# Turned key sums on column tiles in their own PSUM bank, one copy for both output banks, and input loads that begin one step earlier

## Chip, cores and metric

The kernel runs on one core of one Trainium2 chip. The metric is the device time of one execution in microseconds (us); lower is better. Three runs of the kernel before gave 825.5, 828.97 and 832.24 us, median 828.97.

## What is computed

Linear attention over 8 sequences, 8 heads, 576 tokens and 64 channels, followed by a layer that sends each token to one of 8 experts. The attention part, which is the part the change touches:

```
def phi(x):
    proj = einsum('bhsd,df->bhsf', x, w_phi)              # 64 -> 128 features
    proj = proj - max(abs(proj), axis=-1)
    return concat([exp(proj), exp(-proj)], axis=-1)       # 256 features
q_p, k_p = phi(q), phi(k)
kv  = einsum('bhsf,bhsd->bhfd', k_p, v)
z   = sum(k_p, axis=2)
out = einsum('bhsf,bhfd->bhsd', q_p, kv) / (einsum('bhsf,bhf->bhs', q_p, z)[..., None] + 1e-6)
```

Then x is the output with the heads side by side (512 channels). The logits of a token are x @ w_gate (8 experts) and its local gate is x @ w_local (1 column). The expert e is the argmax of the logits, or the expert of the token before where the local gate is 0.5 or more; the output row is p[e] * (relu(x @ w1[e]) @ w2[e]).

## The kernel before

**Tiling.** The work of the attention is cut into 16 units (a pair of sequences and a pair of heads), each of 9 chunks of 128 tokens, 144 chunks in all; two chunks make a pair, 72 pairs. Chunk 4 of a unit holds the end of one sequence and the start of the next, so a unit has two sums of keys and values (`kvp`), one for each sequence: 32 sums.

**Rounds.** After a short head (pairs 0 to 2) and one step for pair 3 alone (`step`), `round` (lines 676 to 718) runs 34 times on two pairs, a and b (`cur`), while it finishes the two pairs of the round before (`prev`). TensorE's order is the order in which this function is written. In one round TensorE does:

1. `qtr` of prev's first pair: turns its projected queries into `tq`; `products` of pair a into `pj` (line 423); `qtr` of prev's second pair.
2. The turns: for each sum that was finished since the last round, four transposes (`halves`, line 448) of its 128 value columns `kvs[:, sg, MID]` into columns 256 to 383 of the `pj` tile that pair b will be written to (`fb`), and VectorE copies them out as `ks` (line 527).
3. `products` of pair b into that tile.
4. `sums` of prev's first pair (lines 479, 493) into `kvp`.
5. `num` (line 568) twice: the output of two finished pairs, one after the other, into the two banks of one tile `nm` of two banks. After each, ScalarE copies its bank to `nx` (line 573), VectorE makes the reciprocals `rc` (lines 575, 576), GpSimd multiplies into `xo` (line 578) and adds the gate columns to `lg` (lines 587 to 590), and SyncE writes `xo` to the tensor `xs` in HBM (line 593).
6. The gates of the sums turned in step 2: `ks` times `wgi` (line 535) into columns 256 to 291 of pair a's `pj` tile (`fa`), copied by ScalarE into nine columns at each end of `kvs` (line 537). Only after this is a sum ready for `num`.
7. `sums` of prev's second pair. When a sum has its fifth part, `kv_end` has ScalarE copy it from `kvp` to `kvs` (lines 514, 515).

Between these stand `chores`: steps of the routing (`gate`), of a table, and of the first experts' weights, whose halves ScalarE casts (line 644) and GpSimd subtracts (line 646) in the last ten rounds or so.

**The other engines in a round.** VectorE: for each of a and b a maximum (line 430) and a subtraction (line 432), about 1.2 us each. ScalarE: four exponentials of `tq` (`qexp`, line 462), then four of the keys (line 440), two for the pair b of the round before and two for pair a. ScalarE's place for the copies at high priority is chosen by the scheduler.

**PSUM.** `pj` has two tiles (`psf`), `kvp` two (`pskv`), and `tq` and `nm` share one tile of two banks (`psb`, one buffer): `qtr` of the next round waits until `nm` has been copied out, and `num` until `qexp` has read `tq`.

**Loads.** Keys and queries come in `kq` (four buffers) and values in `v` (five), three chunks to a load. Groups 0 to 3 are asked for at the start, the rest is a list `loads` in the order keys, queries, values. `paced_load` issues one of them per chunk, four per round, each held on SyncE's queue until a given matmul is done:

```
if self.loads and NBP * NHP * NC - 12 - len(self.loads) < at - 4:
    self.hold(self.loads.pop(0)(), behind)
```

The first is popped in the first round (at = 8), so load number k (from 0) goes out at chunk k + 8 and belongs to group 4 + k // 3, whose first chunk is 12 + 3 (k // 3): keys go out four chunks ahead of the products that read them, queries three.

**After the rounds.** `last_turns` and `last_sums` (lines 720 to 757) finish the last two pairs and the outputs that are left; then the expert part runs, about 430 us of it, in which TensorE is busy nearly all the time.

Of the kernel before, what the change touches and what calls it, by code (L numbers as in the profile page):

```python
# [21 lines left out]
TB = 2 * S  # L22
# [44 lines left out]
class Kernel:  # L67
# [9 lines left out]
    def run(self):  # L77
        nc, tc, A = self.nc, self.tc, self.A
        act, dve = self.act, self.dve
        with ExitStack() as root:  # L80
# [49 lines left out]
            with tc.manual_schedule(engines={mybir.EngineType.PE}):  # L130
                self.head()
                self.step(HEAD)
                pairs = ExitStack()
                self.psb = self.mkpool(pairs, "psb", 1, "left", PSUM)
                prev = (HEAD,)
                for p in range(HEAD + 1, n // 2, 2):
                    if p == FILL + 4:
                        self.background.append(self.table())
                    self.round((p, p + 1), prev)
                    prev = p, p + 1  # L140
                turn = self.last_turns(prev)
            pairs.close()
            self.psb = self.mkpool(back, "psb", 2, "left", PSUM)
            self.tail = True
            with tc.manual_schedule(engines={mybir.EngineType.PE}):
                self.last_sums(prev, turn)
            for x in self.background:
                for _ in x:
                    pass
# [35 lines left out]
    def fill(self, k):  # L185

        a, b = 17 * k // 4, 17 * (k + 1) // 4
        if k == 0:
            self.empty = self.back2.tile([128, 17, PLACE], F32, name="empty", tag="xo", bufs=4)
# [318 lines left out]
    def kv_end(self, u, b, t):  # L508


        hp = u % NHP
        kvs = self.back2.tile([128, 2, 2 * (KV + D + 1)], F32, name="kvs", bufs=4)
        with self.tc.high_priority():
            self.act.copy(kvs[:, :, MID].rearrange("p s (h d) -> p s h d", h=2), t[:, :, :, 0:D])
            self.act.copy(kvs[:, :, DEN], t[:, :, :, D])
        e = {}
# [12 lines left out]

        def gate(t):  # L530

            g = t[:, 0, 256:292].rearrange("p (s h e) -> p s h e", s=2, h=2)
            for sg in (0, 1):
                for r in (slice(0, 64), slice(64, 128)):
                    self.pe.matmul(g[r, sg], e["ks"][:, sg, r], self.wgi[:, hp], start=True, stop=True)
            with self.tc.high_priority():
                self.act.copy(kvs.rearrange("p s (h x) -> p s h x", h=2)[:, :, :, 0:9], g)
            self.kvb[u, b] = kvs
            self.gated.add((u, b))
            while self.pair < NBP * NHP * NC // 2 and self.batches(2 * self.pair) | self.batches(2 * self.pair + 1) <= self.gated:  # L540
                self.ready.append(self.pair)
                self.pair += 1
        self.turns.append(turn)
# [3 lines left out]
        u, c = divmod(i, NC)  # L547
        return {(u, int(c > 4)), (u, int(c > 3))}

    def num(self, t):  # L550

        if not self.ready:
            return
        dve, pool = self.dve, self.pool
        j = self.ready.pop(0)
        t = t[:, 0:4 * KV].rearrange("p (c k) -> p c k", c=2)
        spans = []
        for z in (0, 1):
            u, c = divmod(2 * j + z, NC)
            qp = self.ch.pop(2 * j + z)["qp"]  # L560
            spans.append((u, c, slice(z, z + 1)))
# [8 lines left out]
        if spans[0][0] == spans[1][0]:  # L570
            spans = [(u, spans[0][1], slice(0, 2))]
        nx = self.back2.tile([128, 2, 2 * KV], F32, name="nx", bufs=2)
        self.act.copy(nx, t)  # L573
        rc = self.back2.tile([128, 2, 2], F32, name="rc", bufs=3)
        dve.tensor_scalar_add(rc, nx[:, :, DEN], 1e-6)
        dve.reciprocal(rc, rc)
        xo = self.back2.tile([128, 2, 2 * KV], F32, name="xo", bufs=4)
        pool.tensor_mul(xo.rearrange("p c (h k) -> p c h k", h=2), nx.rearrange("p c (h k) -> p c h k", h=2),  # L578
                        rc.unsqueeze(3).broadcast_to([128, 2, 2, KV]))
        for u, c, z in spans:  # L580
            bp, hp = divmod(u, NHP)
            n = z.stop - z.start
            if hp == 0 and c == 0:
                self.lg[bp] = self.back2.tile([128, NC, 9], F32, name="lg")
            lg, ga, gb = self.lg[bp][:, c:c + n], xo[:, z, 0:9], xo[:, z, 2 * KV - 9:2 * KV]
# [5 lines left out]
            r0 = bp * TB + c * 128  # L591
            dst = self.xs[r0:r0 + n * 128, hp * 128:hp * 128 + 128].rearrange("(c p) d -> p c d", p=128)
            self.sp.dma_start(dst, xo[:, z, MID])
            if c + n == NC and hp == NHP - 1:
                self.ends(bp)

# [53 lines left out]

    def sums(self, p):

        for i in sorted((2 * p, 2 * p + 1), key=lambda i: i % NC != 4):
            if i % NC == 4:
                self.kv4(i)
            else:
                self.kv(i)

    def step(self, p):

        exps = self.proj(p)
        exps()
        pj = self.ch[2 * p - 2]["pj"]
        self.qtr(p - 1, pj)
        self.qexp(p - 1, pj)
        self.sums(p - 1)
        self.exps = lambda: None

    def ask(self):

        if self.asked:
            self.asked()
            self.hold(self.marks[self.sp], self.last_num)
            self.asked = None

    def round(self, cur, prev):

# [7 lines left out]
        fa, fb = [x.rearrange("p h c j f -> p h (c j f)") for x in (ta, tb)]  # L685
# [29 lines left out]
        if prev[1:]:  # L715
            self.sums(prev[1])
        self.paced_load(2 * b + 1, self.last_sum)
        self.ask()

    def last_turns(self, prev):  # L720

        t = self.psb.tile([128, 2, 512], F32, name="tq", tag="nm")
        for k, p in enumerate(prev):
            self.qtr(p, t, 256 * k)
        pj = self.psf.tile([128, 2, 512], F32, name="pj")
        turns, self.turns = self.turns, []
        for x in [x(pj) for x in turns]:
            x(pj)
# [4 lines left out]
        self.sums(prev[0])  # L733
        return pj

    def spread(self, n):
        for _ in range(n):
            self.num(self.psb.tile([128, 512], F32, name="nm"))

    def last_sums(self, prev, pj):  # L740

        self.spread(1)
        gates, self.gates = self.gates, []
        for x in gates:
            x(pj)
        self.chores()
        self.sums(prev[1])
        self.spread(2)
        t = self.psf.tile([128, 2, 512], F32, name="pj")
        turns, self.turns = self.turns, []  # L750
        for x in [x(t) for x in turns]:
            x(t)
        self.spread(max(len(self.ready) - 1, 0))
        gates, self.gates = self.gates, []
        for x in gates:
            x(t)
        self.spread(len(self.ready))

    def chores(self):
# [1007 lines left out]
```

## Time and profile before

| | |
|---|---|
| median of 3 runs | 828.97 us (825.5 to 832.24) |
| the profiled execution | 830.83 us |
| its span in the profile | 829.1 us, so 1.73 us lie around the span |
| TensorE busy | 735.1 us, 89% of the span |
| VectorE, ScalarE, GpSimd busy | 477.0, 364.5, 286.0 us |
| the 34 rounds | from 15.9 to 384.6 us |
| the expert part | from 399.5 us to the end |

A busy share is a mean over stages with different limits; the rounds and the expert part have to be read apart. In the timeline a row merges neighbouring instructions of one kind: start, length in us, engine, line, operation, output and inputs, count, and in brackets the idle time before and what ended it. PEld is TensorE loading its stationary operand, which overlaps its matmuls.

### The profile page before, as it was taken

The page shows a single profiled execution, that of the slowest core. Times are in us where ns is not written, and L with a number is a line of the kernel's source. Part 1 is how long each engine was busy: PE and PEld are TensorE (multiplying, and loading weights), DVE is VectorE, ACT ScalarE, POOL GpSimd, SP SyncE. Part 2 cuts the span into 40 slices and gives each one's busy share as a digit, 9 for nine tenths or more (in the row PEclk, how much of TensorE's full clock was granted, in tenths as well). Part 3 has the DMA queues.
Part 4 walks back from the last instruction along what each step waited for, and adds up shares of the span by engine and source line. Part 5 has one row for each costly group of instructions (what it writes and reads, how often), then busy time and mean ns, then how long its engine had stood idle before and what let it go on. Part 6 is the DMA issues. An engine that isn't in the chain of part 4 may idle for free. (4 is left out here: it accounts for less than half of the span.)

```text
span 829.1 us, 22143 instructions
## 1 busy us (share of the span) xinstructions
PE 735.1 (89%) x9193; PEld 641.0 (77%) x9193; DVE 477.0 (58%) x862; ACT 364.5 (44%) x736; POOL 286.0 (34%) x448
## 2 busy tenths in 40 slices
PE   8678778778777777768999999999999999999997
PEld 7567777777677676668889888957897889788895
DVE  6454655764566655775675547265557556563520
ACT  5444554564455565456243533163333424342420
POOL 1202221244312464656774515240415142432011
PEclk9888999999899898999999999999999999999999
DMA  4633333343333454554343859986477558665630
GB/s 139 205 82 88 112 104 103 105 124 87 99 104 105 113 158 135 168 159 137 80 156 110 300 137 327 339 311 194 147 194 238 126 196 203 193 165 153 190 128 36
DMA packets 101143, 129.53 MB, mean 156 GB/s; under 512 B 41938, under 2 KB 80274, under 8 KB 100990
## 3 DMA queue, kind: packets, MB, share of 16 engines
q1 hardware_dynamic: 92560, 105.10, 43.5%
q0 software_dynamic: 8032, 22.78, 8.1%
q8 instruction: 73, 1.20, 0.6%
q14 instruction: 30, 0.25, 0.1%
q10 hardware_dynamic: 448, 0.20, 0.1%
HBM read 98.12 MB, written 21.80 MB: 145 GB/s over the span
## 5 line engine op out<-in xcount | busy, mean ns | idle before, releaser
L423 PE MATMUL pj<-first,kq 64*128 64x128 f32 x1120 | 94.5, 304 | 59.5 <-DVE ks L527 39.2
L430 DVE TENSOR_REDUCE m<-pj 128x8 f32<-128x1024 f32 x70 | 85.7, 1224 | 83.1 <-PE pj L423 82.2
L423 PEld LDWEIGHTS pj<-first,kq 64*128 64x128 f32 x1120 | 76.7, 201 | 69.2 <-DVE ks L527 43.3
L1458 PE MATMUL l<-xhi,whi 128*128 128x352 f32 (+5 forms) x352 | 124.1, 353 | 0.2 <-DVE hl L1505 0.2
L1460 PE MATMUL l<-xhi,wlo 128*128 128x352 f32 (+5 forms) x352 | 123.6, 351 | 0.0
L1459 PE MATMUL l<-xlo,whi 128*128 128x352 f32 (+5 forms) x352 | 123.4, 351 | 0.0
L1504 ACT ACTIVATE hh<-l 128x384 fp32r<-128x384 f32 (+4 forms) x88 | 45.0, 511 | 166.3 <-PE l L1460 166.1
L1282 DVE TENSOR_TENSOR wlo<-wraw,whi 128x1024 fp32r<-128x1024 f32 x80 | 99.9, 1265 | 29.0 <-ACT whi L1279 28.9
L568 PE MATMUL nm<-kvs,qp 128*64 128x74 f32 x2304 | 93.9, 238 | 21.7 <-ACT nx L573 20.4
L1458 PE MATMUL l<-whi,hh 128*128 128x512 f32 (+1 forms) x288 | 112.7, 391 | 0.0
L1459 PE MATMUL l<-wlo,hh 128*128 128x512 f32 (+1 forms) x288 | 112.3, 390 | 0.0
L1460 PE MATMUL l<-whi,hl 128*128 128x512 f32 (+1 forms) x288 | 112.2, 390 | 0.0
L1505 DVE SCALAR_TENSOR_TENSOR hl<-l,hh 128x384 fp32r<-128x384 f32 (+4 forms) x88 | 51.1, 580 | 102.8 <-ACT hh L1504 102.8
L568 PEld LDWEIGHTS nm<-kvs,qp 128*64 128x64 f32 x2304 | 85.4, 145 | 27.5 <-ACT nx L573 25.3
L578 POOL TENSOR_TENSOR xo<-nx,rc 128x296 f32<-128x296 f32 x72 | 49.0, 681 | 149.5 <-ACT nx L573 75.2
L462 ACT ACTIVATE qp<-tq 128x512 f32<-128x512 f32 x138 | 71.3, 602 | 65.3 <-PE tq L448 65.2
L1279 ACT CAST whi<-wraw 128x1024 fp32r<-128x1024 f32 x80 | 81.7, 1045 | 20.3 <-PE l L1460 12.8
L432 DVE TENSOR_TENSOR sb<-pj,m 128x1024 f32<-128x1024 f32 x70 | 85.5, 1221 | 3.7
L479 PE MATMUL kvp<-v,kp 128*64 128x65 f32 x2048 | 86.4, 243 | 0.0
L479 PEld LDWEIGHTS kvp<-v,kp 128*64 128x64 f32 x2048 | 76.3, 155 | 6.1 <-issue 2.2
L440 ACT ACTIVATE kp<-sb 128x512 f32<-128x512 f32 x140 | 78.2, 649 | 2.8 <-DVE sb L432 2.7
L1574 POOL DMA_INDIRECT out<-y,p_tokm x32 | 39.8, 1243 | 108.5 <-DVE y L1570 97.7
(273 smaller groups left out, 1065.1 us busy)
## 6 DMA issues: line engine op xcount, KB each, us to landing
wraw<-in_w1h SPq DMA_DIRECT2D x40, 512.0 KB, 4.9
wraw<-in_w2h SPq DMA_DIRECT2D x40, 512.0 KB, 4.5
kq<-in_kqT SPq DMA_DIRECT2D x88, 192.0 KB, 2.7
v<-in_va SPq DMA_DIRECT2D x48, 195.0 KB, 2.8
xs<-xo SPq DMA_DIRECT2D x64, 128.0 KB, 2.2
whi<-in_w2h SPq DMA_DIRECT2D x8, 512.0 KB, 5.5
wlo<-in_w2h SPq DMA_DIRECT2D x8, 512.0 KB, 6.2
wraw<-in_w1h SPq DMA_DIRECT2D x8, 256.0 KB, 2.8
```

The lines of the kernel that those rows point to most:

```text
L423: self.last_pe = self.pe.matmul(t[:, h, i % 2, j, :], kq[r, j, s], self.w2[r], start=True, stop=True)
L430: dve.tensor_reduce(m, f, AX.X, ALU.max, apply_absolute_value=True)
L432: self.last_dve = dve.tensor_sub(sb.rearrange("p h c j f -> p (h c j) f"), f, m.unsqueeze(2).broadcast_to([128, 8, 128]))
L440: self.last_act = act.activation(kp[:, :, :, sg, :].rearrange("p c h f -> p h c f"), sb[:, :, :, 0], AF.Exp, scale=1.0 - 2 * sg)
L462: self.last_act = self.act.activation(qp[:, sg].rearrange("p h (c r k) -> p (h c) r k", c=2, r=2), src, AF.Exp, scale=1.0 - 2 * sg)
L479: self.last_sum = self.pe.matmul(t[r, sg, h], kp[:, h, sg, r], v[:, h], start=first and sg + h == 0, stop=last and sg + h == 2)
L568: self.last_num = self.pe.matmul(t[r, z, k], qp[:, sg, h, q], self.kvb[u, int(c > 4 - x)][:, sg, k], start=sg == 0, stop=sg == 1)
L1279: self.act.copy(hi, raw)
L1282: (low or self.dve).tensor_sub(lo[:, c], raw[:, c], hi.bitcast(F32)[:, c])
L1458: mm(o, ah, bh, start=first, stop=False)
L1459: mm(o, ah, bl, start=False, stop=False)
L1460: self.last_pe = mm(o, al, bh, start=False, stop=last)
```

## The change

- `turn` writes the turned sum into the sum's own `kvp` bank, columns 0 to 255 (line 524 of the new kernel): four matmuls of `kvs` against the identity, each with all 128 partitions in and 64 out, in place of four transposes into pair b's `pj` tile. ScalarE, not VectorE, copies it to `ks` (line 526).
- `gate` writes into the same bank (line 534), and ScalarE copies from there (line 536).
- In a round, `turn` and `gating` now stand at two places each: turns behind `products` of b, with their gates behind the sums of prev's first pair; and turns behind the first `num`, with their gates behind the second.
- `num` only does the matmuls. A new `numbers` empties both banks of `nm` with one ScalarE copy straight into `xo` (592 elements, line 574), makes the reciprocals of both pairs at once, multiplies in place on GpSimd, and issues the write to `xs` ahead of the additions to `lg`. `nx` is gone; `xo` has three buffers of four chunks in place of four of two.
- The two chunks of prev's second pair are summed with the chores between them.
- `step` issues three loads, held behind its products; the pacing rule is as it was, so each later load goes out three chunks earlier (load k at chunk k + 5).
- `last_turns` and `last_sums` follow the same order.

```diff
-        def turn(t):
+        def turn():
+            ks = e["ks"] = self.back2.tile([128, 2, 128], F32, name="ks")
             for sg in (0, 1):
-                self.halves(t, 256 + sg * 64, kvs[:, sg, MID])
+                for x in (0, 1):
+                    r = slice(64 * x, 64 * x + 64)
+                    self.pe.matmul(o[r, sg * 128:sg * 128 + 128], kvs[:, sg, MID][:, r], self.ident, start=True, stop=True)
+            with self.tc.high_priority():
+                self.act.copy(ks.rearrange("p s k -> p (s k)"), o[:, 0:256])
             self.gates.append(gate)
-            return copy
-
-        def copy(t):
-            e["ks"] = self.back2.tile([128, 2, 128], F32, name="ks")
-            with self.tc.high_priority():
-                self.dve.tensor_copy(e["ks"].rearrange("p s (r k) -> p s r k", r=2),
-                                     t[:, :, 256:384].rearrange("p r (s k) -> p s r k", s=2))
-
-        def gate(t):
-
-            g = t[:, 0, 256:292].rearrange("p (s h e) -> p s h e", s=2, h=2)
+
+        def gate():
+
+            g = o[:, 0:36].rearrange("p (s h e) -> p s h e", s=2, h=2)
...
-        nx = self.back2.tile([128, 2, 2 * KV], F32, name="nx", bufs=2)
-        self.act.copy(nx, t)
...
+    def numbers(self, t, js):
...
+        xo = self.back2.tile([128, 4, 2 * KV], F32, name="xo", bufs=3)[:, 0:2 * w]
+        self.act.copy(xo.rearrange("p (n c) k -> p n (c k)", n=w), t[:, 0:w, 0:4 * KV])
+        rc = self.back2.tile([128, 4, 2], F32, name="rc", bufs=3)[:, 0:2 * w]
...
+        pool.tensor_mul(x, x, rc.unsqueeze(3).broadcast_to([128, 2 * w, 2, KV]))
...
     def step(self, p):
 
         exps = self.proj(p)
         exps()
+        for _ in range(3):
+            self.hold(self.loads.pop(0)(), self.last_pe)
...
         self.paced_load(2 * a, self.last_pe)
         for p in prev[1:]:
             self.qtr(p, t, 256)
-        turns, self.turns = self.turns, []
-        for x in [x(fb) for x in turns]:
-            x(fb)
         self.products(b, tb)
...
-        self.sums(prev[0])
+        self.turn()
+        for x in self.sums(prev[0]):
+            x()
         self.paced_load(2 * a + 1, self.last_sum)
-        t = self.psb.tile([128, 2, 512], F32, name="nm")
-        self.num(t[:, 0])
+        self.gating()
+        t, js = self.psb.tile([128, 2, 512], F32, name="nm"), []
+        self.num(t, js)
         self.paced_load(2 * b, self.last_sum)
+        self.turn()
...
-        self.num(t[:, 1])
-        gates, self.gates = self.gates, []
-        for x in gates:
-            x(fa)
+        self.num(t, js)
+        self.numbers(t, js)
+        self.gating()
+        sums = self.sums(prev[1]) if prev[1:] else []
+        for x in sums[:1]:
+            x()
```

On TensorE, one round in the steady part of the kernel before, from `qtr` (`tq`) to the last sums:

```order
L448 MATMUL tq<-first,sb 128x64 x8
L423 MATMUL pj<-first,kq 128x128 x8
L448 MATMUL tq<-first,sb 128x64 x8
L448 MATMUL pj<-first,kvs 128x64 x4
L423 MATMUL pj<-first,kq 128x128 x8
L479 MATMUL kvp<-v,kp 64x65 x16
L568 MATMUL nm<-kvs,qp 64x74 x32
L535 MATMUL pj<-wgi,ks 64x18 x4
L479 MATMUL kvp<-v,kp 64x65 x16
```

In the changed kernel 14 rounds read as follows; here they are called rounds of form A (a sum was finished in the second half of the round before):

```order
L448 MATMUL tq<-first,sb 128x64 x8
L423 MATMUL pj<-first,kq 128x128 x8
L448 MATMUL tq<-first,sb 128x64 x8
L423 MATMUL pj<-first,kq 128x128 x8
L524 MATMUL kvp<-first,kvs 64x128 x4
L479 MATMUL kvp<-v,kp 64x65 x16
L534 MATMUL kvp<-wgi,ks 64x18 x4
L565 MATMUL nm<-kvs,qp 64x74 x32
L479 MATMUL kvp<-v,kp 64x65 x16
```

Another 14 have the turn between the two `num` and the gate behind them, form B (a sum was finished in the first half of this round, or just at its end); from `qtr` of the second pair on:

```order
L448 MATMUL tq<-first,sb 128x64 x8
L423 MATMUL pj<-first,kq 128x128 x8
L479 MATMUL kvp<-v,kp 64x65 x16
L565 MATMUL nm<-kvs,qp 64x74 x16
L524 MATMUL kvp<-first,kvs 64x128 x4
L565 MATMUL nm<-kvs,qp 64x74 x16
L534 MATMUL kvp<-wgi,ks 64x18 x4
L479 MATMUL kvp<-v,kp 64x65 x16
```

Four rounds have neither turn nor gate, and the first two of the 34 are special. So the turn has moved from ahead of pair b's products to behind them, and its gate stands one to three rows behind it in the same round.

On ScalarE, one round of the kernel before, from `qexp` to the copy of the gates:

```order
L462 ACTIVATE qp<-tq 128x512 x4
L440 ACTIVATE kp<-sb 128x2x2x128 x4
L514 COPY kvs<-kvp 128x2x128
L515 COPY kvs<-kvp 128x2x2
L573 COPY nx<-nm 128x296 x2
L537 COPY kvs<-pj 128x4x9
```

The same stretch of a round of form A in the changed kernel:

```order
L462 ACTIVATE qp<-tq 128x512 x4
L440 ACTIVATE kp<-sb 128x2x2x128
L526 COPY ks<-kvp 128x256
L440 ACTIVATE kp<-sb 128x2x2x128 x2
L536 COPY kvs<-kvp 128x4x9
L440 ACTIVATE kp<-sb 128x2x2x128
L574 COPY xo<-nm 128x592
L514 COPY kvs<-kvp 128x2x128
L515 COPY kvs<-kvp 128x2x2
```

And of a round of form B, where lines 514 and 515 have more or fewer of the four key exponentials ahead of them from round to round:

```order
L462 ACTIVATE qp<-tq 128x512 x4
L440 ACTIVATE kp<-sb 128x2x2x128 x2
L514 COPY kvs<-kvp 128x2x128
L440 ACTIVATE kp<-sb 128x2x2x128
L515 COPY kvs<-kvp 128x2x2
L440 ACTIVATE kp<-sb 128x2x2x128
L526 COPY ks<-kvp 128x256
L574 COPY xo<-nm 128x592
L536 COPY kvs<-kvp 128x4x9
```

ScalarE has taken over the copy of `ks`, and its place among the key exponentials is now in the path from turn to gate.

## Rows read from the trace of the kernel before

**Rows 1.** Windows by stage: length, busy time of each engine, granted clock, DMA.

```profile
36.32:70.51 34.19, 26.05 (x537) 23.32 (x534) 17.36 (x31) 15.80 (x37) 4.42 (x12) 0.85 0.35 101
70.51:375.08 304.57, 237.01 (x5469) 216.51 (x5465) 190.26 (x369) 162.57 (x388) 113.42 (x251) 0.92 0.41 119
...
399.53:829.00 429.47, 422.78 (x2132) 356.68 (x2129) 235.69 (x409) 153.53 (x236) 146.25 (x128) 1.00 0.62 188
```

**Rows 2.** What TensorE waited for: us in total, times, longest.

```profile
PE pj L423 <- DVE ks L527: 39.2, 30, 1.5
PE nm L568 <- ACT nx L573: 20.4, 31, 2.0
PE pj L423 <- DMA kq<-in_kqT: 20.2, 22, 2.4
```

**Rows 3.** TensorE's timeline of one round with a turn and no late load.

```profile
173.26 0.46 PE L448 MATMUL tq<-first,sb 64*128 64x64 f32 x8
...
174.75 0.29 PE L448 MATMUL pj<-first,kvs 64*128 64x64 f32 x4
176.34 1.16 PE L423 MATMUL pj<-first,kq 64*128 64x128 f32 x16 [1.29 <-DVE ks L527]
177.43 1.15 PE L479 MATMUL kvp<-v,kp 128*64 128x65 f32 x32
178.41 1.20 PE L568 MATMUL nm<-kvs,qp 128*64 128x74 f32 x32
180.17 1.25 PE L568 MATMUL nm<-kvs,qp 128*64 128x74 f32 x32 [0.56 <-ACT nx L573]
181.25 0.36 PE L535 MATMUL pj<-wgi,ks 128*64 128x18 f32 x8
181.54 0.70 PE L493 MATMUL kvp<-v,kp 64*64 64x65 f32 x32
...
182.78 0.40 PE L448 MATMUL tq<-first,sb 64*128 64x64 f32 x6
```

**Rows 4.** Timeline of TensorE and ScalarE in one round without a turn.

```profile
204.92 0.46 PE L448 MATMUL tq<-first,sb 64*128 64x64 f32 x8
...
206.61 2.07 ACT L462 ACTIVATE qp<-tq 128x512 f32<-128x512 f32 x4 [2.18 <-PE tq L448]
...
207.45 0.70 PE L493 MATMUL kvp<-v,kp 64*64 64x65 f32 x32
...
208.54 1.17 ACT L440 ACTIVATE kp<-sb 128x512 f32<-128x512 f32 x2
...
209.58 0.39 ACT L514 COPY kvs<-kvp 128x256 f32<-128x256 f32 x1
...
210.36 0.20 ACT L515 COPY kvs<-kvp 128x4 f32<-128x4 f32 x1
...
211.43 1.25 PE L568 MATMUL nm<-kvs,qp 128*64 128x74 f32 x32 [1.45 <-ACT nx L573]
...
213.54 0.46 PE L448 MATMUL tq<-first,sb 64*128 64x64 f32 x8
```

**Rows 5.** Timeline of the next round, which waits for a load.

```profile
216.61 0.72 PE L423 MATMUL pj<-first,kq 64*128 64x128 f32 x8 [1.29 <-DVE ks L527]
...
219.09 1.34 PE L423 MATMUL pj<-first,kq 64*128 64x128 f32 x8 [1.76 <-DMA kq<-in_kqT]
```

**Rows 6.** Windows: behind that wait, and a round with a turn and no late load.

```profile
219.09:223.20 4.11, 4.11 (x58) 3.85 (x60) 2.45 (x2) 0.81 (x3) 0.00 (x0) 0.50 0.01 2
...
268.98:278.50 9.52, 7.67 (x209) 7.11 (x206) 7.41 (x19) 5.28 (x14) 4.60 (x10) 1.00 0.44 122
```

**Rows 7.** Groups of instructions by line, 15 to 400 us: busy, mean ns, idle before.

```profile
L578 POOL TENSOR_TENSOR xo<-nx,rc 128x296 f32<-128x296 f32 x70 | 47.7, 681 | 149.5 <-ACT nx L573 75.2 <-DVE rc L576 30.0 <-ACT g_es L800 15.4
L573 ACT COPY nx<-nm 128x296 f32<-128x296 f32 x72 | 29.4, 408 | 87.0 <-PE nm L568 84.6 <-POOL wlo L646 1.8 <-POOL lg L589 0.5
L646 POOL TENSOR_TENSOR wlo<-wraw,whi 128x256 fp32r<-128x256 f32 x32 | 22.5, 729 | 0.4 <-ACT whi L644 0.3
L527 DVE COPY ks<-pj 128x256 f32<-128x256 f32 x32 | 13.3, 416 | 2.0 <-PE pj L448 2.0
L514 ACT COPY kvs<-kvp 128x256 f32<-128x256 f32 x32 | 12.1, 377 | 21.3 <-PE kvp L479 19.3 <-PE kvp L493 1.5
```

More of the change, by code (lines that the diff above doesn't have):

```diff
@@ L140, in run @@
                     prev = p, p + 1
-                turn = self.last_turns(prev)
+                self.last_turns(prev)
             pairs.close()
@@ L145, in run @@
             with tc.manual_schedule(engines={mybir.EngineType.PE}):
-                self.last_sums(prev, turn)
+                self.last_sums(prev)
             for x in self.background:
@@ L188, in fill @@
         if k == 0:
-            self.empty = self.back2.tile([128, 17, PLACE], F32, name="empty", tag="xo", bufs=4)
+            self.empty = self.back2.tile([128, 17, PLACE], F32, name="empty", tag="xo", bufs=3)
             self.pool.memset(self.empty, 0.0)
@@ L560, in num @@
             qp = self.ch.pop(2 * j + z)["qp"]
-            spans.append((u, c, slice(z, z + 1)))
             for h in (0, 1):
@@ L569, in num @@
                                                        start=sg == 0, stop=sg == 1)
-        if spans[0][0] == spans[1][0]:
-            spans = [(u, spans[0][1], slice(0, 2))]
-        nx = self.back2.tile([128, 2, 2 * KV], F32, name="nx", bufs=2)
-        self.act.copy(nx, t)
-        rc = self.back2.tile([128, 2, 2], F32, name="rc", bufs=3)
-        dve.tensor_scalar_add(rc, nx[:, :, DEN], 1e-6)
-        dve.reciprocal(rc, rc)
-        xo = self.back2.tile([128, 2, 2 * KV], F32, name="xo", bufs=4)
-        pool.tensor_mul(xo.rearrange("p c (h k) -> p c h k", h=2), nx.rearrange("p c (h k) -> p c h k", h=2),
-                        rc.unsqueeze(3).broadcast_to([128, 2, 2, KV]))
+    def numbers(self, t, js):
+        if not js:
+            return
+        dve, pool, w = self.dve, self.pool, len(js)
+        xo = self.back2.tile([128, 4, 2 * KV], F32, name="xo", bufs=3)[:, 0:2 * w]
+        self.act.copy(xo.rearrange("p (n c) k -> p n (c k)", n=w), t[:, 0:w, 0:4 * KV])
+        rc = self.back2.tile([128, 4, 2], F32, name="rc", bufs=3)[:, 0:2 * w]
+        dve.tensor_scalar_add(rc, xo[:, :, DEN], 1e-6)
+        dve.reciprocal(rc, rc)
+        x = xo.rearrange("p c (h k) -> p c h k", h=2)
+        pool.tensor_mul(x, x, rc.unsqueeze(3).broadcast_to([128, 2 * w, 2, KV]))
+        spans = []
+        for z in range(2 * w):
+            u, c = divmod(2 * js[0] + z, NC)
+            if c == 0 or z == 0:
+                spans.append([u, c, slice(z, z)])
+            spans[-1][2] = slice(spans[-1][2].start, z + 1)
         for u, c, z in spans:
@@ L651, in sums @@
     def sums(self, p):
[L653 to L657, printed above, removed]
+        return [lambda i=i: (self.kv4 if i % NC == 4 else self.kv)(i)
+                for i in sorted((2 * p, 2 * p + 1), key=lambda i: i % NC != 4)]
     def step(self, p):
@@ L665, in step @@
         self.qexp(p - 1, pj)
-        self.sums(p - 1)
+        for x in self.sums(p - 1):
+            x()
         self.exps = lambda: None
@@ L674, in ask, with turn, gating @@
             self.asked = None
+    def turn(self):
+        turns, self.turns = self.turns, []
+        for x in turns:
+            x()
+    def gating(self):
+        gates, self.gates = self.gates, []
+        for x in gates:
+            x()
     def round(self, cur, prev):
@@ L684, in round @@
         ta, tb = [self.psf.tile([128, 2, 2, 2, 128], F32, name="pj") for _ in cur]
-        fa, fb = [x.rearrange("p h c j f -> p h (c j f)") for x in (ta, tb)]
+        fa = ta.rearrange("p h c j f -> p h (c j f)")
         self.products(a, ta)
@@ L708, in round @@
         self.exps = self.feature(b, tb)
-        self.num(t[:, 1])
-        gates, self.gates = self.gates, []
-        for x in gates:
-            x(fa)
+        self.num(t, js)
[3 more added lines that the diff above has]
+        for x in sums[:1]:
+            x()
         self.small_ps = [fa[:, r, 384:512] for r in (1, 0)]
         self.chores()
-        if prev[1:]:
-            self.sums(prev[1])
+        for x in sums[1:]:
+            x()
         self.paced_load(2 * b + 1, self.last_sum)
@@ L724, in last_turns @@
             self.qtr(p, t, 256 * k)
[L725 to L728, printed above, removed]
         for k, p in enumerate(prev):
@@ L732, in last_turns, with last_sums @@
             self.exps()
-        self.sums(prev[0])
-        return pj
+        self.turn()
+        for x in self.sums(prev[0]):
+            x()
+        self.gating()
     def spread(self, n):
         for _ in range(n):
-            self.num(self.psb.tile([128, 512], F32, name="nm"))
-    def last_sums(self, prev, pj):
+            t, js = self.psb.tile([128, 1, 512], F32, name="nm"), []
+            self.num(t, js)
+            self.numbers(t, js)
+    def last_sums(self, prev):
         self.spread(1)
-        gates, self.gates = self.gates, []
-        for x in gates:
-            x(pj)
+        self.turn()
         self.chores()
[L747 to L752, printed above, removed]
+        self.spread(1)
+        self.gating()
+        for x in self.sums(prev[1]):
+            x()
+        self.spread(1)
+        self.turn()
         self.spread(max(len(self.ready) - 1, 0))
-        gates, self.gates = self.gates, []
-        for x in gates:
-            x(t)
+        self.gating()
         self.spread(len(self.ready))
```

15 lines of the change are left out of this document (8 added, 7 removed).

## The prediction

> **What bounds the kernel now.** I read the windows by stage first, then TensorE's waits, then the timeline of single rounds. The expert part has TensorE busy 422.8 of 429.5 us at full clock [rows 1]: the change touches nothing there, and I cost it at nothing. In the rounds TensorE is busy 237.0 of 304.6 us, ScalarE 162.6, VectorE 190.3 and GpSimd 113.4: no engine is full, so the rounds are bound by what TensorE waits for. Three waits hold nearly all of it: products of pair b for `ks` (39.2 us, 30 times), `num` for the copy of the `num` before (20.4 us, 31 times), products for a late load of keys or queries (20.2 us, 22 times) [rows 2]. They sum to 79.8 us of the 368.7 that the rounds take.
>
> A round without a late load shows where they stand [rows 3]: from 173.26 to 182.78, 9.52 us, with 1.29 idle between the turn and pair b's products and 0.56 between the two `num`. A round without a turn takes 8.62 us, 1.45 of it between the `num` [rows 4]. A late load costs more than its wait. Behind a wait of 1.76 us that followed one of 1.29 [rows 5], the granted clock was 0.50 for the next 4.1 us, TensorE's level of 1.2 GHz, against 1.00 in a round without a late load [rows 6]. Over the rounds the mean clock is 0.92 in 304.6 us and 0.85 in the 34.2 before [rows 1]; with two levels, 1.0 and 0.5, that is 48.7 and 10.3 us at the lower, and half of it, at most 29.5 us, is lost.
>
> **What goes.** (1) The turn no longer writes pair b's tile, so pair b's products don't wait for `ks`: 39.2 us. (2) Nothing copies between the two `num`: 20.4 us. (3) Each load goes out three chunks, three quarters of a round, earlier. A load issued at the end of a round is then due not in the next round but in the one behind it, some 6 us or more later, against waits of at most 2.4 us [rows 2]. I keep 3 us of the 20.2 for the first rounds, where the start is still filling: 17 us. (4) Most of the lower clock hangs on those waits. I take 18 of the 29.5 us as recovered; the bounds are 0 and 29.5. Together 94.6 us.
>
> **What comes.** I lay out the new rounds from durations of the old. TensorE's first part (both `qtr`, both products) ends 2.53 us into a round without a turn (207.45 less 204.92), and `qexp` runs there from 1.69 to 3.76 [rows 4].
>
> Form A: turn to 2.8, sums of prev's first pair (0.98, from 177.43 to 178.41 [rows 3]) to 3.8. The gates need `ks`, which stands on ScalarE behind `qexp` and one key exponential. Two of these take 1.17 us [rows 4], from 3.62 on, so with a pitch of some 0.52 the copy begins at 4.14 and, at 0.377 as line 514 for the same 256 elements [rows 7], ends near 4.5. The gates begin at 4.57: a wait of 0.76, with two `num` and the last sums queued behind it. Gates 0.3, two `num` 2.2 (1.08 each, 180.17 to 181.25 [rows 3]), sums 1.0: 8.1 us. The first `num` of these rounds uses sums gated earlier; the second uses the sum just gated, whose copy (line 536, behind two more exponentials) ends at 5.6, before the second begins at 6.0. The copy of both banks, which the next `qtr` waits for, takes some 0.65 us (an estimate from 0.377 for 256 and 0.408 for 296 elements and 2.07 for four of 512 [rows 4, 7]) and ends at 7.8, beneath the last sums.
>
> Form B: sums to 3.55, the first `num` waits for `qexp` to 3.8 and ends at 4.9. The turn waits for line 515, which stood 5.64 us into the round in the same order of exponentials (210.36 + 0.20 - 204.92 [rows 4]): 0.8 us more. Turn, second `num`, gates, sums: 8.4 us, and 7.9 or 8.9 where line 514 has fewer or all exponentials ahead. Rounds without a turn: 0.25 of wait, 7.05 us.
>
> New waits: 14 x 0.76 + 14 x 1.05 + 4 x 0.25, and some 3 us in the two first rounds: 29 us. Bounds: 10 us, if the copies run as soon as TensorE is done, and 55, if each waits for all four exponentials (1 us more in 28 rounds).
>
> Late rounds: there ScalarE's casts stand in front of the copy of both banks or of `ks`, and GpSimd has 32 subtractions of 0.73 us [rows 7] beside a multiplication that is now twice 0.68 in one piece. I add 6 us; bounds 0 and 15.
>
> At nothing: VectorE loses the 13.3 us of `ks` [rows 7], which ended only the wait of (1). GpSimd's one multiplication starts later, so the write to `xs` goes out some 1.7 us into the next round, with that round's loads behind it on SyncE's queue; the three chunks of (3) cover this, and without that cover the late loads come back. The turned matmuls: four transposes of 64 columns took 0.29 us; 16 products of 128 columns took 1.09 to the next row [rows 3], so four products' worth is 0.27 us, the same.
>
> Against this stands a rule of the Trainium skill (TensorEngine Tiling (Array Packing), Restrictions): column tiling excludes the transpose mode for fp32. TensorE: Matmul & The Clock Gate, Terms, calls that mode four times faster for fp32. By that rule the turns would cost four times 0.29 us, and the sum would be 28 us less; the trace does not agree, since per column the transposes ran no faster than the products. It stands among the rivals.
>
> **The sum.** Gone 94.6, come 29 + 6: 60 us off the profiled execution's span of 829.1, so 769.1, or 770.8 with the 1.73 us around it. That execution (830.83) lies 0.2% above the median of 828.97; scaled by that, 769 us. A cross-check from the other side: 14 x 8.1 + 14 x 8.4 + 4 x 7.05 + 16.4 for the first two is 275.6 us for rounds that take 368.7. That would be 93 us, if no round were disturbed by clock, routing or loads; today's would be 31 x 9.52 + 3 x 8.62 = 321 undisturbed and lose 48 to these; I expect about 33 of it to remain or come.
>
> **Rivals.**
> - *The copies on ScalarE become the wait.* Its queue is in order, and the turn's way now passes it three times (515, 526, 536) in one round. If each turn finds all four exponentials ahead, the 55 stand for the 29, and with some 9 us of clock not recovered the gain is 25 to 34: about 799 us. For: form B has rounds in that order, and late rounds have casts there too. Against: form A, half of the rounds, has only one exponential ahead. From 0.9 us of further wait per turn this decides.
> - *The loads stay late.* If the start three chunks earlier is eaten by SyncE's queue, 17 and 18 us stay: a gain of 25, 804 us. For: the write to `xs` goes out later. Against: the next use is a whole round away.
> - *The turned matmuls are dear.* If four of them take four times the 0.29 us of the transposes [rows 3], 32 turns cost 28 us more: a gain of 32, 797 us. Against: the pace of the products, 0.27 us for four. The rule on the transpose mode above speaks for it.
> - *Slower: the clock falls in every round.* The new waits lie close together behind the sums. If each of 34 rounds draws a stretch at 1.2 GHz, as the one in [rows 5, 6], and it covers all 7 us of TensorE's work in the round, 3.5 us are lost in each: 119 in place of 29.5. With 76.6 gone by (1) to (3) and 35 come, that is 829 + 90 - 42 = 877 us. It decides from 4.1 us at the lower level in each round, where the loss eats the 42. For: two waits in a row did it [rows 5]. Against: rounds with 1.29 and 0.56 us idle in 9.5 keep a clock of 1.00 [rows 6], and the new ones have no more than 1.1 in 8.4. The Trainium skill speaks for this rival (TensorE: Matmul & The Clock Gate, A second HAM failure mode): short idles between groups of matmuls can make the clock swing between its levels. [...]
> - *More is gained:* the clock recovers wholly and the late rounds cost nothing, 78 us or more: 736 to 750.
>
> **Chances.** Forecast (750 to 788 us) 0.60; more gained 0.10; ScalarE 0.15; loads 0.07; dear turns 0.03; slower 0.05. About 1% (8 us) is what a measurement of this kernel can tell from no change. Faster by more 0.92, within it 0.03 (part of the ScalarE case at its worst), slower 0.05. The range 746 to 800 leaves out most of the further gain, the upper part of the loads and ScalarE cases and the slower one, some 2 in 10.
>
> **What would show it.** In the profile after: no wait of line 423 for `ks`; none between two `num` in one round; waits for `kq` of a few us, all early; a mean clock in the rounds of 0.96 or more; new waits of line 534 for line 526 of 0.7 us and of line 524 for line 515 of 0.8 us, about 14 of each; rounds of 8.1 to 8.9 us; the expert part 430 us as before. I am wrong if gates or turns wait 1.7 us or more, if the waits for `kq` stay above 10 us, if the clock stays below 0.93, or if the expert part grows because weights or lists come too late for its earlier start.

## The result, and the profile after

The changed kernel takes 748.84 us (median of 4 runs, 747.89 to 751.27) beside 828.81 us for the kernel before: 0.9039 of its time, 95% interval 0.8997 to 0.9082. That is 20 us under the forecast of 769, inside the range of 746 to 800, and just inside the case called "more is gained" (736 to 750), which had a chance of 0.10.

The page of the changed kernel, TensorE's busy time and the granted clock in 40 slices:

```profile
PE 714.5 (96%) x9321; PEld 625.8 (84%) x9321; DVE 452.7 (61%) x764; ACT 367.5 (49%) x735; POOL 271.2 (36%) x367
...
PEclk9999999999999999999999999999999999999999
```

Windows by stage of the changed kernel (length, busy us of TensorE, its loads, VectorE, ScalarE, GpSimd, then granted clock, DMA share, GB/s), the first five rounds, the later ones but the last, and the expert part:

```profile
15.89:56.91 41.02, 34.66 (x873) 32.24 (x874) 26.10 (x35) 25.69 (x58) 9.05 (x18) 1.00 0.57 175
56.91:296.33 239.42, 221.74 (x5569) 205.52 (x5566) 173.11 (x288) 165.05 (x386) 104.87 (x187) 1.00 0.53 154
...
318.63:746.90 428.27, 422.77 (x2133) 356.60 (x2129) 233.97 (x408) 153.59 (x236) 144.09 (x126) 1.00 0.63 189
```

The expert part is as it was, 428.3 us against 429.5 [rows 1]. The gain lies in the 34 rounds. As one window each, the kernel before and the changed one:

```profile
15.89:384.60 368.71, 283.98 (x6461) 258.95 (x6462) 225.78 (x422) 192.88 (x456) 128.53 (x283) 0.92 0.41 121
```

```profile
15.89:304.79 288.90, 264.39 (x6645) 245.25 (x6646) 204.66 (x330) 196.21 (x455) 118.25 (x214) 1.00 0.53 156
```

The rounds are 79.8 us shorter: TensorE is idle 24.5 us in place of 84.7, which is 60.2, and busy 19.6 us less. The second part is the clock, 1.00 in place of 0.92, less what the turned matmuls cost (below). What TensorE waits for in the changed rounds (us in total, times, longest):

```profile
PE kvp L524 <- ACT kvs L515: 11.4, 12, 1.7
PE kvp L534 <- ACT ks L526: 5.8, 12, 0.6
PE nm L565 <- ACT kvs L536: 1.3, 1, 1.3
PE kvp L534 <- issue: 0.9, 2, 0.5
PE tq L448 <- ACT xo L574: 0.8, 1, 0.8
```

All three waits of [rows 2] are gone: no line has `kq`, `nx`, or line 423 behind `ks`. The new ones, with some small lines, sum to 22.7 us.

TensorE's timeline of one round of form A, 7.96 us from `qtr` to `qtr` where the round of [rows 3] takes 9.52:

```profile
81.09 0.47 PE L448 MATMUL tq<-first,sb 64*128 64x64 f32 x8
...
82.34 0.41 PE L448 MATMUL tq<-first,sb 64*128 64x64 f32 x8
82.58 1.11 PE L423 MATMUL pj<-first,kq 64*128 64x128 f32 x16
83.62 0.66 PE L524 MATMUL kvp<-first,kvs 128*64 128x128 f32 x8
84.11 1.10 PE L479 MATMUL kvp<-v,kp 128*64 128x65 f32 x32
85.68 0.41 PE L534 MATMUL kvp<-wgi,ks 128*64 128x18 f32 x8 [0.47 <-ACT ks L526]
85.93 2.25 PE L565 MATMUL nm<-kvs,qp 128*64 128x74 f32 x64
...
89.05 0.46 PE L448 MATMUL tq<-first,sb 64*128 64x64 f32 x8
```

Pair b's products follow `qtr` at once, and the two `num` are one row of 64 without a pause. What is left is the gates' wait for `ks`, whose copy ScalarE makes behind `qexp` and one key exponential:

```profile
82.78 2.06 ACT L462 ACTIVATE qp<-tq 128x512 f32<-128x512 f32 x4 [1.01 <-PE tq L448]
84.71 0.65 ACT L440 ACTIVATE kp<-sb 128x512 f32<-128x512 f32 x1
85.23 0.39 ACT L526 COPY ks<-kvp 128x256 f32<-128x256 f32 x1
```

In form B the turn's wait depends on how many key exponentials stand ahead of lines 514 and 515 on ScalarE: none in the round from 97.52 to 105.48 with two ahead of line 515 (7.96 us), 0.63 in the one from 89.05 with three (8.47), and 1.28 with all four, in the round from 105.48 (9.75):

```profile
109.29 1.25 PE L565 MATMUL nm<-kvs,qp 128*64 128x74 f32 x32
111.82 0.66 PE L524 MATMUL kvp<-first,kvs 128*64 128x128 f32 x8 [1.28 <-ACT kvs L515]
```

The copy of both banks, among ScalarE's groups of instructions by line from 15 to 320 us (busy, mean ns):

```profile
L574 ACT COPY xo<-nm 128x592 f32<-128x592 f32 x33 | 21.6, 655 | 26.0 <-issue 18.4 <-PE nm L565 5.8 <-POOL wlo L652 1.7
```

### The profile page after: what moved, and what is told of

It reads as the page before. It is cut to its first block, busy times and chain, and to the rows that moved or that the text cites. A ratio compares the mean times of both kernels' runs of the same rounds, so it can differ in the third digit from the quotient of the medians.

```text
span 746.9 us, 22108 instructions
## 1 busy us (share of the span) xinstructions
PE 714.5 (96%) x9321; PEld 625.8 (84%) x9321; DVE 452.7 (61%) x764; ACT 367.5 (49%) x735; POOL 271.2 (36%) x367
## 5 line engine op out<-in xcount | busy, mean ns | idle before, releaser
L565 PE MATMUL nm<-kvs,qp 128*64 128x74 f32 x2304 | 87.2, 229 | 4.0 <-ACT kvs L536 1.3
L579 POOL TENSOR_TENSOR xo<-xo,rc 128x592 f32<-128x592 f32 (+1 forms) x39 | 43.0, 1102 | 123.6 <-ACT xo L574 41.9
L565 PEld LDWEIGHTS nm<-kvs,qp 128*64 128x64 f32 x2304 | 79.6, 136 | 8.2 <-ACT qp L462 3.3
L440 ACT ACTIVATE kp<-sb 128x512 f32<-128x512 f32 x140 | 83.3, 660 | 1.4 <-DVE sb L432 1.2
L423 PE MATMUL pj<-first,kq 64*128 64x128 f32 x1120 | 77.7, 279 | 0.0
L479 PE MATMUL kvp<-v,kp 128*64 128x65 f32 x2048 | 77.0, 224 | 0.6 <-issue 0.6
L1475 PEld LDWEIGHTS l<-xhi,whi 128*128 128x128 f32 x352 | 66.1, 188 | 7.0 <-issue 0.8
L479 PEld LDWEIGHTS kvp<-v,kp 128*64 128x64 f32 x2048 | 68.1, 137 | 4.3 <-issue 1.1
```

What stands on the lines that cost most here:

```text
L423: self.last_pe = self.pe.matmul(t[:, h, i % 2, j, :], kq[r, j, s], self.w2[r], start=True, stop=True)
L440: self.last_act = act.activation(kp[:, :, :, sg, :].rearrange("p c h f -> p h c f"), sb[:, :, :, 0], AF.Exp, scale=1.0 - 2 * sg)
L479: self.last_sum = self.pe.matmul(t[r, sg, h], kp[:, h, sg, r], v[:, h], start=first and sg + h == 0, stop=last and sg + h == 2)
L1475: mm(o, ah, bh, start=first, stop=False)
```

## Experiments

The theory was the sum of the prediction: four causes, each worth its wait. The rivals were that a part is worth nothing until another is there, that ScalarE is the wrong engine for `ks`, and that the turned matmuls cost time. Each kernel was timed four times (the turns alone ten times) beside the kernel before, whose medians beside the result and in the three groups of runs were 828.81, 830.10, 828.72 and 823.81 us. So kernels are compared by their ratios to it; a difference in us is the difference of ratios times 829.

**The three parts, alone and in pairs.** "Loads" is the kernel before with three lines more:

```diff
         exps = self.proj(p)
         exps()
+        for _ in range(3):
+            self.hold(self.loads.pop(0)(), self.last_pe)
```

> The kernel before with nothing changed but the three loads in the one-pair step. Theory (late loads cost their wait and the lower clock behind it): the waits of products for keys and queries fall from 20.2 us to under 5, the mean granted clock of the rounds rises from 0.92 to 0.97 or more, the time falls by 35 to 45 us to some 790. Rival (the clock hangs on the waits for the turned sums and between the two outputs): the waits for loads go, the clock stays near 0.92, the time falls by some 18 us to 811. Rival (the loads stay late behind the writes on SyncE's queue): under 8 us gained.

Measured: 785.6 us, ratio 0.9477 (0.9407 to 0.9547), 43 us less. The wait for `kq` is gone and the others stay (39.5 and 23.6 us). Its 34 rounds as one window:

```profile
15.90:341.02 325.12, 255.35 (x6477) 236.58 (x6473) 227.65 (x423) 192.33 (x459) 128.29 (x284) 0.99 0.48 137
```

The rounds are 43.6 us shorter: TensorE is busy 255.35 us there in place of 283.98, 28.6 less, at a clock of 0.99, and idle 69.8 in place of 84.7. Three issues early in the program bring more than half of the whole gain, two thirds of it by the clock: the stretches at the lower level were almost wholly the work of the late loads.

"Copy" is the kernel before with the new `num` and `numbers`, `xo` in three buffers of four chunks, and nothing else:

```diff
-            self.num(t[:, 0])
+            self.num(t, js)
...
-            self.num(t[:, 1])
+            self.num(t, js)
+            self.numbers(t, js)
```

> The kernel before with nothing changed but the one copy of both output banks straight into xo. Theory (the wait between the two outputs is on the path, and late loads take part of it back because each round is shorter): the 20.4 us of waits are gone, the waits for loads grow to 25 us or more, the time falls by 8 to 16 us to some 817. Rival (the parts add up): 20 us gained, 809.

Measured: 811.59 us, ratio 0.9818 (0.9729 to 0.9906), 15 us less (8 to 22 by that interval). The wait for `nx` (20.4) is gone, and of that 3.8 us came back in the wait for loads:

```profile
PE pj L423 <- DVE ks L527: 40.1, 30, 1.5
PE pj L423 <- DMA kq<-in_kqT: 24.0, 19, 2.8
```

"Turns" is the kernel before with the new `turn` and `gate` at their two new places, and with the chores between the two sums of prev's second pair:

```diff
-        turns, self.turns = self.turns, []
-        for x in [x(fb) for x in turns]:
-            x(fb)
         self.products(b, tb)
...
+        self.turn()
```

> The kernel before with nothing changed but the turned sums and gates in the sum's own bank and their new places. Theory: 39.2 us of waits for the turned sums go, some 20 us of new waits come (turn for the copy of the sum, gate for the copy of the turned sum), and late loads take back most of the rest: 5 to 15 us gained, some 819. Rival (the parts add up): 20 us gained, 809. Rival (the new waits and the lower clock eat it): no gain.

Measured: 831.68 us, ratio 1.0016 (0.9976 to 1.0057): nothing, below the 5 to 15 us of the theory, though the largest wait of [rows 2] is gone. Its waits:

```profile
PE pj L423 <- DMA kq<-in_kqT: 52.8, 24, 4.0
PE nm L567 <- ACT nx L572: 16.1, 23, 1.4
PE kvp L524 <- ACT kvs L515: 5.0, 8, 0.6
PE kvp L534 <- ACT ks L526: 2.9, 6, 0.6
```

The wait for loads has grown by 32.6 us, to 52.8. In its timeline pair b's products start right behind `qtr`, and stop:

```profile
104.76 0.41 PE L448 MATMUL tq<-first,sb 64*128 64x64 f32 x8
105.00 0.44 PE L423 MATMUL pj<-first,kq 64*128 64x128 f32 x4
108.09 0.94 PE L423 MATMUL pj<-first,kq 64*128 64x128 f32 x12 [2.65 <-DMA kq<-in_kqT]
```

So the wait for `ks` stood in front of the wait for the loads and covered it: without the one the other grew. The clock in the rounds stays at 0.93 (15.90 to 389.17 us). That the loads are not the whole of it the pairs show: with the loads in time the same edits bring 7 to 9 us, and not 39.

Pairs: loads and copy together, then the changed kernel without its early loads, then turns and loads without the copy.

> The kernel before with the one copy and the early loads, the turns as they were. Theory: the waits for the turned sums (39 us) stay, those between the outputs and for loads are gone and the clock is near 1.0: 20 + 40 us gained, some 769. Rival (the clock needs the turns moved as well): some 785.

Measured: 757.09 us, ratio 0.9148 (0.9079 to 0.9217), 12 us below what was expected. Of the three waits `ks` alone is left, at its old size, and the clock in the rounds is 1.00. Wait, and rounds as a window:

```profile
PE pj L423 <- DVE ks L527: 40.1, 30, 1.5
...
15.90:310.24 294.34, 248.40 (x6453) 232.85 (x6451) 213.28 (x358) 187.21 (x424) 113.44 (x203) 1.00 0.52 150
```

So the turns, with all their edits, are worth 0.0109, or 9 us, on top of this kernel. In the rounds TensorE is idle 45.9 us here and 24.5 in the changed kernel, but busy 248.4 against 264.4, both at a clock of 1.00: what the shorter waits give, the turn takes back in large part as work. Its price follows below.

```diff
         exps()
-        for _ in range(3):
-            self.hold(self.loads.pop(0)(), self.last_pe)
```

> The changed kernel without the three early loads. Theory (late loads and the clock behind them are what a shorter round runs into): waits for keys and queries of 30 us or more, mean clock of the rounds below 0.93, 800 us or more. Rival (the loads are a small part, and the pacing takes care of itself): waits of some 20 us and no lower clock, some 770.

Measured: 813.52 us, ratio 0.9817 (0.9769 to 0.9864), clock in the rounds 0.91 (15.90 to 369.18 us), as expected. The waits for `ks` and `nx` are gone, but the wait for loads has grown by 27 us, and lines 524 and 534 wait 9.4 us in their place:

```profile
PE pj L423 <- DMA kq<-in_kqT: 47.2, 30, 4.3
```

The early loads, 43 us alone, are worth 0.0778, or 64 us, here.

> The changed kernel with each output bank copied by itself, as before. Theory: the waits between the two outputs come back, 20 us in rounds with no turn between them and less where the turn stands between; 12 to 20 us slower than the changed kernel, 761 to 769. Rival (the turn between the outputs hides the copy): under 5 us slower.

Measured: 778.71 us, ratio 0.9399 (0.9341 to 0.9457), some 10 to 18 us above what was expected. The wait between the `num` is there, and the waits of the turn much as in the changed kernel:

```profile
PE nm L567 <- ACT nx L572: 22.4, 24, 1.6
PE kvp L524 <- ACT kvs L515: 9.8, 11, 1.5
PE kvp L534 <- ACT ks L526: 7.8, 16, 0.6
```

The copy is worth 15 us alone and 30 us here (0.9399 less 0.9039). In the rounds that is 21.8 us less idle and 7.0 less busy: the clock was 0.98 (15.90 to 333.59 us) and is 1.00. All eight versions, as us below the kernel before by their ratios, the corners of a cube: nothing 0, turns -1, copy 15, turns and copy 15, loads 43, turns and loads 50, copy and loads 71, all 80. Each ratio is uncertain by 0.4 to 0.9%, so differences of less than some 8 us between two of them mean little: the 7 us of the turns behind the loads may be noise, their 9 us on top of copy and loads stand just outside it, and the step from 15 to 80 far outside.

**Which engine copies `ks`.** The changed kernel with that copy on VectorE:

```diff
-                self.act.copy(ks.rearrange("p s k -> p (s k)"), o[:, 0:256])
+                self.dve.tensor_copy(ks.rearrange("p s k -> p (s k)"), o[:, 0:256])
```

> The changed kernel with the copy of the turned sum on VectorE in place of ScalarE. Theory (the gates wait for ScalarE's queue): the 6.4 us of waits of the gates go, nothing else moves: 742 us. Rival (VectorE's reduction and subtraction stand in front of it and wait behind it): 749 us or more.

Measured: 761.38 us, ratio 0.9179 (0.9131 to 0.9227), 0.0140 or 12 us more than with ScalarE, as the rival had it. The gates' wait for `ks` is 22.6 us in the whole span. In VectorE's timeline the copy stands behind a maximum, a subtraction and a second maximum, though its source was ready some 1.8 us before (four turned matmuls began at 79.31 and the next row at 79.80):

```profile
79.50 1.22 DVE L432 TENSOR_TENSOR sb<-pj,m 128x1024 f32<-128x1024 f32 x1
80.65 1.21 DVE L430 TENSOR_REDUCE m<-pj 128x8 f32<-128x1024 f32 x1
81.78 0.41 DVE L526 COPY ks<-kvp 128x256 f32<-128x256 f32 x1
```

So "ScalarE is the wrong engine" falls for this place in the round, where ScalarE has smaller pieces ahead of the copy (0.52 us against 1.2).

**What the turned matmuls cost.** The changed kernel with each of them issued twice, the second writing the same result again:

```diff
-                    self.pe.matmul(...)
+                    for _ in (0, 1):
+                        self.pe.matmul(...)
```

> The changed kernel with the four turned matmuls of each sum issued twice, the same result written again. One set takes 0.48 us from its start to the next row. Theory (in form A the wait of the gates hides it, in form B it is on the path): 14 x 0.48 = 7 us slower, 756. Rival (on the path everywhere): 32 x 0.48 = 15 us slower, 764. Rival (hidden everywhere): no change, 749.

Measured: 763.05 us, ratio 0.9200 (0.9157 to 0.9243), 0.0161 or 13 us more, the number of the rival "on the path everywhere". The row of eight and the row behind it in one round of form A:

```profile
79.80 1.15 PE L525 MATMUL kvp<-first,kvs 128*64 128x128 f32 x16
80.72 1.15 PE L479 MATMUL kvp<-v,kp 128*64 128x65 f32 x32
```

From 79.80 to 80.72 are 0.92 us, where the four of the changed kernel take 0.49 (83.62 to 84.11): 0.43 for four, times 32 turns 13.8 us. In form A the scheduler also moved the copy of `ks` behind a second key exponential, so whether a longer turn alone hides under that wait there was not settled by this run.

**The turn at another place.** Copy and loads, with the old transposes into pair b's `pj` tile, and ScalarE in VectorE's place for `ks`:

```diff
-                self.dve.tensor_copy(e["ks"].rearrange("p s (r k) -> p s r k", r=2),
+                self.act.copy(e["ks"].rearrange("p s (r k) -> p s r k", r=2),
```

> The kernel of copy and loads with ScalarE copying the turned sums, nothing moved on TensorE. The copy stands behind one exponential of the queries. Theory: the wait per turn falls from 1.29 to about 0.9 us, 13 us faster than copy and loads, 744. Rival (the exponentials behind the copy delay the outputs as much): no change, 757.

Measured: 740.43 us, ratio 0.8987 (0.8954 to 0.9019), 0.0161 or 13 us less than with VectorE; its wait for `ks` is 24.8 us in place of 40.1. This is at the changed kernel's 0.9039 or a little under it without touching the turn's data.

Then, besides, the turns are moved ahead: behind products a, with the second `qtr` behind them (first diff) or with both `qtr` behind them (second diff, against the first), so that TensorE has work while ScalarE copies.

```diff
         self.products(a, ta)
         self.paced_load(2 * a, self.last_pe)
-        for p in prev[1:]:
-            self.qtr(p, t, 256)
         turns, self.turns = self.turns, []
         for x in [x(fb) for x in turns]:
             x(fb)
+        for p in prev[1:]:
+            self.qtr(p, t, 256)
         self.products(b, tb)
```

> As the run before, but with the first turned queries ahead of pair a's products and the second behind the turns. Theory: products wait 0.2 to 0.3 us per turn, 8 us in all; some 731. Rival: as in the run before.

Measured: 730.56 us, ratio 0.8858 (0.8821 to 0.8895); the wait for `ks` is 6.8 us in 29, the longest 0.8.

```diff
-        self.qtr(prev[0], t)
         self.products(a, ta)
...
+        self.qtr(prev[0], t)
         for p in prev[1:]:
             self.qtr(p, t, 256)
         self.products(b, tb)
```

> The kernel of copy and loads (turns by transposes into pair b's tile, gates at the round's end, as before), with a round that begins with pair a's products, then the turns, then both turned queries, and with ScalarE copying the turned sums. Theory (the wait for the turned sums was one of place: the copy stood behind VectorE's reduction, and ScalarE is idle ahead of its exponentials of the queries): waits of pair b's products fall from 40 us to under 5, no new waits of turn and gate come, 30 us faster than copy and loads, some 727. Rival (the exponentials of the queries start later and the outputs wait for them): 10 us faster at most, 747 or more.

Measured: 725.22 us (724.57 to 726.27), ratio 0.8806 (0.8773 to 0.8839). It beats both kernels. Its 34 rounds, as a window, and TensorE in one of them:

```profile
15.21:278.23 263.02, 251.22 (x6466) 235.32 (x6463) 210.37 (x329) 196.77 (x456) 111.44 (x202) 0.99 0.57 168
```

```profile
108.30 1.16 PE L423 MATMUL pj<-first,kq 64*128 64x128 f32 x16
109.29 0.28 PE L448 MATMUL pj<-first,kvs 64*128 64x64 f32 x4
109.41 0.67 PE L448 MATMUL tq<-first,sb 64*128 64x64 f32 x16
110.04 1.16 PE L423 MATMUL pj<-first,kq 64*128 64x128 f32 x16
```

ScalarE, at the same place, copies `ks` while it would otherwise wait for `qtr`:

```profile
109.62 0.37 ACT L527 COPY ks<-pj 128x256 f32<-128x256 f32 x1 [2.13 <-PE pj L448]
```

It had been idle for 2.13 us; the copy begins 0.33 us after the first of the transposes and is done at 109.99, before pair b's products begin at 110.04. The wait disappears into time that ScalarE had free, and no turn waits in its stead; the largest waits left are those of small products of the routing (3.1 us once, 2.5 in three). TensorE is idle 11.8 of 263.0 us. Against the changed kernel's rounds that is 12.7 us less idle and 13.2 less busy, the second mostly because the turns are transposes again.

## Why the prediction was right, and where it was off

**The account.** From the kernel before to the changed one the rounds lose the three waits of [rows 2] (79.8 us) and, taken from the same list, some small lines of 5 us; they get 22.7 us of waits. That is 62 us less idle by the list and 60.2 by the windows. The clock gives back some 29.5 us, which the prediction worked out as the bound for the rounds from 36.32 to 375.08 us, and the turned matmuls take 32 x (0.49 - 0.12) = 11.8 us more: TensorE's busy time should fall by 17.7, and fell by 19.6. Together 80 us by the terms, 79.8 by the windows.

**(1) `ks`, 39.2 us: right in the profile, not a gain by itself.** The line is gone. But the turns alone brought nothing, and the turns on top of copy and loads 9 us: of the 40.1 us, 17.2 came back in the two new waits and up to 11.8 in the matmuls, which leaves 11. The prediction added this wait and that for the loads as if each stood alone; the sum was right only because the same change also moved the loads. It had also left some 10 us of this wait, by new waits of 29 and matmuls at nothing. That this net came out is luck: the waits were 12 us too large in it, and the matmuls 12 too small.

**(2) `nx`, 20.4 us: right.** No `num` waits for the one before. The copy of both banks, estimated at 0.65 us, took 655 ns.

**(3) and (4) Loads and clock: the mis-sized terms.** The prediction kept 3 us of the 20.2 and took 18 of the 29.5 us for the clock. Both went wholly: no wait for `kq`, and a clock of 1.00 (at least 0.96 was forecast). That is 3 + 11.5 us of the 20 by which the forecast was too slow. The step that was off is "Most of the lower clock hangs on those waits. I take 18 of the 29.5 us as recovered": nearly all of it did, as the run with the loads alone shows (TensorE 28.6 us less busy, clock 0.99).

**New waits: the mechanism right, the size too large.** 29 and 6 us were forecast, 22.7 came in all. In form A the layout held to the hundredth: the copy of `ks` was to begin 4.14 us into the round and the gates at 4.57; they began at 4.14 (85.23 less 81.09) and 4.59. The wait was 0.47 and not 0.76: the turn before it took 0.49 us and not 0.27, and the trace counts idle time from the end of the row before (1.10 us for the sums), where the prediction counted from their 0.98 us to the next row. Over all the new waits that difference in counting is some 3 us, an estimate from 0.12 for each. A round took 7.96 (8.1 forecast), the three rounds of form B shown above 7.96, 8.47 and 9.75 (7.9 to 8.9). 35 less 22.7 is 12 us of the miss; with the 14.5 above and the 5 of small waits that went, the terms were 32 us too pessimistic, and the next one 12 us too optimistic.

**"At nothing: the turned matmuls" was wrong.** The prediction held 0.29 us for four transposes against 0.27 for four products. Both are misread. 0.29 is the length of the row, and the next row can start well before a row's end: from start to start four transposes take 0.12 us (109.29 to 109.41 in the kernel with the turn first). And "16 products" are 8 instructions: a row of the trace counts each of these fp32 matmuls twice, as the order of the instructions shows beside it (x8 there, x16 in [rows 3]). Eight products in 1.09 us make 0.55 for four, and 0.49 was measured. So the factor is 4 (0.49 to 0.12), half of it from 128 columns in place of 64 and half from the pace per column.

The rule of the Trainium skill that the prediction set aside (TensorEngine Tiling (Array Packing), Restrictions, with TensorE: Matmul & The Clock Gate, Terms) thus agrees with the trace in kind: without the transpose mode the turn became dearer. Per column the runs show a factor of 2, where the Trainium skill says 4 without naming what it compares. Perfetto Trace Analysis, Transposes, in the Trainium skill, asks for the transpose mode where a transpose is meant; the fastest kernel here does so.

**The rivals.** *ScalarE's copies become the wait*: seen in single rounds (1.28 us with four exponentials ahead), 17.2 us in all for lines 515 and 526, and not 55. *The loads stay late*: did not happen, but without their early start they would have been worse than forecast, 47.2 us and not 20. *The turned matmuls are dear*: right on the factor of 4, wrong on the price, 11.8 us and not 28, because it multiplied 0.29. *Slower by the clock*: fell; rounds with waits of 0.47, 0.63 or 1.28 us keep 1.00. *More is gained*: this is what happened, by its first condition; the late rounds did cost something, the last six 8.98 us each (250.89 to 304.79) against 8.42 in the 26 before (from 32.06).

**The expert part**: 428.3 us, as forecast.

## What to carry to other kernels

A wait in the list is worth its time only if nothing else is late behind it: before a wait is costed, look at when the operands of the waiting instruction land, and when rounds get shorter, start the loads earlier by as much first (here 43 us alone, 64 us once the rounds had shrunk). For a short copy in the path, look for a place where its engine is idle and the waiting engine has other work, before the data are moved elsewhere: a few lines exchanged and another engine brought 0.0342 (28 us) on top of copy and loads, the new bank 0.0109 (9 us). The price of a row of matmuls is read from its start to the next row's start, and its count held against the program.

## What the runs showed of the hardware that was not expected

- Four fp32 transposes of 64 columns take 0.12 us to the next row, four column-tiled fp32 matmuls of 128 columns 0.49, and eight of these 0.92. In the trace a matmul of this kind stands as two instructions (x8 for four), a transpose as one (x4 for four).
- The clock's lower level hung almost wholly on the waits for loads. With 39.5 us of waits for `ks` and 23.6 for `nx` in the rounds the granted clock is 0.99 (loads alone), and in the four kernels with loads waited for 20.2 to 52.8 us it is 0.91 to 0.93. Waits of up to 1.7 us, the longest for line 515, left it at 1.00 in every stage of the changed kernel. TensorE: Matmul & The Clock Gate, A second HAM failure mode, in the Trainium skill, tells of a kernel in which frequent short idles between groups of matmuls make the clock swing; here it is 0.98 or more as a mean of the rounds in every kernel without late loads.
